# Attention and up-projection on four 32-row groups of TensorE, in an order written by a planner

## The chip, the core and the metric

The kernel runs on one core of a Trainium2 chip. A core has five engines that work side by side, each through its own queue in order: TensorE (PE in the profile; PEld is its weight load), VectorE (DVE), ScalarE (ACT), GpSimd (POOL) and SyncE (SP, which here only starts transfers). Operands lie in SBUF, 128 partitions wide; matmul results go to PSUM, in banks of 128 x 512 fp32. A matmul has a stationary operand, loaded first (up to 128 rows x 128 columns), and a moving operand that streams past it. The metric is the device time of one launch in microseconds.

## The reference

One sequence of S = 2048 rows, width D = 448, H = 16 heads of 28, hidden width F = 1792, all fp32:

```python
qkv = x @ wqkv                                   # split into q, k, v by head
scores = q @ k^T * 28 ** -0.5
a = (softmax(scores) @ v) @ wo                   # per head, heads side by side
b = (gelu(x @ w_gate) * (x @ w_up)) @ w_down     # tanh form of gelu
g = sigmoid((x * gate_w).sum(-1, keepdims=True))
return g * a + (1 - g) * b
```

Products are taken nearly in fp32: each operand is split into a high part (`hi`, type fp32r) and the rest (`lo`), and hi x hi, hi x lo and lo x hi are added up in PSUM.

## The kernel before

The program has three stages, one after the other on TensorE.

**Stage 1, projections.** x is split into the SBUF tensor `X` (7 blocks of 128 rows: three of hi, three of lo, and one that holds hi and lo of the last 64 rows). q and k are computed transposed, a tile of 128 rows x 512 tokens by 11 matmuls (`PAIRS` lists which block of x meets which block of the weights), evicted as hi and lo and stored to DRAM (`qkd`). Then 16 tiles of v follow (`v_tile`, L209 evicts them on ACT), which stay in SBUF (`VA`).

**Stage 2, attention.** For each head, `Q` and `K` are read back as 4 x 28 rows (hi and lo stacked, so that one product of 114 rows gives all four partial products, with two rows more for a shift of the softmax). A score tile `sc` is 128 keys x 1024 queries: two matmuls of 128 x 512. ACT turns it into `pt` = exp(sc) (L352). A value turn (`values`) multiplies the `pt` of 8 key tiles with 32 columns of v each; four such matmuls stand in the four 32-column groups of the array, one for each quarter of the queries. There are two value turns in each head, 32 in all. Sums `o` are added on DVE (L364, L367). Since exp is slower than the scores, `up()` puts other matmuls between them: x @ w_up, and x @ w_gate for NB = 7 of 14 blocks of 128 hidden columns. Each block is 4 token blocks x 11 matmuls of 128 rows (`ps<-X,half`), evicted by DVE (L410) and stored to DRAM (`ud`). `RATES`, `ENDS` and `LATE` fix by hand how many of them follow each score tile.

When a head's sums are complete, `finish` and `divide` run a chain on POOL's queue: four stores of the denominators (`dend`, L373), one load of them over 128 partitions (`r`, L376), a reciprocal on DVE (L383), its store (`rdend`, L384), four broadcast loads (`rb`, L387), the product o * rb on POOL (L389), and four stores to `od` (L391). Each starts when the one ahead has landed.

**Stage 3, the down projection.** In pairs of hidden blocks and for each 512 tokens: `hidden` forms gelu(gate) * up and splits it into `hl`; `down` multiplies it with the rows of w_down (`pd`, 24 matmuls of 448 columns) and DVE adds the result into `acc` (L514). For the 7 gate blocks that stage 2 left, the gate product is computed here (`pg`, 11 matmuls each); for the others it is loaded from `ud`. Gelu runs on ACT (L494), the product with `u` on DVE (L495), the hi copy on ACT (L496), the rest `lo` on DVE (L497). Rows of w_down are split by `load_f` (L478 on ACT, L479 on DVE). Near the end `load_o` and `project` multiply the attention output with `wo`.

All matmuls go through the helper `mm` (L54), so the profile gives them one line; tiles tell them apart. `pin` keeps an instruction at its place in program order; what is not pinned is placed by the framework's scheduler, but each engine then runs its queue strictly in that order.

Of the kernel before, what the change touches and what calls it, by code (L numbers as in the profile page):

```python
# [25 lines left out]
ENDS = (7, 15)  # L26
LATE = 1
RATES = (2,) * 13 + (1,) * 3
NB = 7
ORDER = (7, 8, 0, 9, 1, 10, 2, 11, 3, 12, 4, 13, 5, 6)  # L30
# [3 lines left out]
NR = 4 * DH + 2  # L34
# [9 lines left out]
PAIRS = [(b, w) for b in range(3) for w in (b, 4 + b)] + [(4 + b, b) for b in range(3)] + [(3, 3), (3, 7)]  # L44


@with_exitstack
def gated_mix(ctx: ExitStack, tc: tile.TileContext, xT, wqk, wvg, wg, wu, wd, wo, sel, ident, out):
# [18 lines left out]
    X = keep.tile([P, 7, S], F32R, name="X")  # L67
    fw = ctx.enter_context(tc.tile_pool(name="fw", bufs=2))
    attn = ctx.enter_context(ExitStack())
    vp = attn.enter_context(tc.tile_pool(name="vp", bufs=1))  # L70
# [6 lines left out]
    halves = {}  # L77

    def load_half(src, f, key, hi, mark=lambda ins: ins):
        raw = fw.tile([P, 4, P], F32, name="hraw", bufs=1)  # L80
        w = fw.tile([P, 8, P], F32R, name="half", bufs=2)
        mark(nc.sync.dma_start(out=raw, in_=src[f]))
        mark(hi(w[:, 0:4], raw))
        mark(nc.vector.tensor_tensor(w[:, 4:8], raw, w[:, 0:4].bitcast(F32), OP.subtract))
        halves[key, f] = w


    with ExitStack() as ph:
        wq = ph.enter_context(tc.tile_pool(name="wq", bufs=1))
        st = ph.enter_context(tc.tile_pool(name="st", bufs=1))  # L90
        wp = ph.enter_context(tc.tile_pool(name="wp", bufs=1))
# [140 lines left out]
        nc.vector.tensor_tensor(sq, sq, sq, OP.mult)  # L232
        for i in range(4):
            v_tile(i)
            if i in (1, 3):

                load_half(wu, i // 2, "u", nc.vector.tensor_copy, pin)
# [6 lines left out]
        for i in range(4, NT):  # L244
            last = v_tile(i)
            if i == NT - 4:
# [19 lines left out]
    kq = attn.enter_context(tc.tile_pool(name="kq", bufs=1, reuse_waits="tile"))  # L266
    heads = [tuple(kq.tile([P, S], F32R, name=f"{x}{i}") for x in "QK") for i in range(2)]
    for Q, K in heads:
        pin(nc.gpsimd.memset(K[96:].bitcast(F32), 1.0))

        pin(nc.gpsimd.memset(Q[96:].bitcast(F32), 0.0))

    def load_q(dst, h):
        for j, a in enumerate((0, 0, 1, 1)):
            nc.sync.dma_start(out=dst[j * DH:(j + 1) * DH].bitcast(F32), in_=qkd[a, h * DH:(h + 1) * DH])

    def load_k(dst, h):
        for j, a in enumerate((0, 1, 0, 1)):
            nc.sync.dma_start(out=dst[j * DH:(j + 1) * DH].bitcast(F32), in_=qkd[a, D + h * DH:D + (h + 1) * DH])

    load_k(heads[0][1], 0)
    load_q(heads[0][0], 0)


    bounded = nc.values_load(flag[0:1, 0:1], min_val=0, max_val=1)
    with tc.If(bounded < 1, label="rows"):
        with ExitStack() as ph:
# [5 lines left out]
            for h in range(H):  # L293
                Q = gp.tile([4 * DH, S], F32R, name="gQ")
                K = gp.tile([4 * DH, S], F32R, name="gK")
                load_q(Q, h)
                load_k(K, h)
# [18 lines left out]
    gp0 = ctx.enter_context(tc.tile_pool(name="gp0", bufs=1, side="right"))  # L316
    def by_act(o, i):
        return nc.scalar.activation(o, i, AF.Copy)


    with ExitStack() as ph:
        pp = ph.enter_context(tc.tile_pool(name="pp", bufs=17))
        op = ph.enter_context(tc.tile_pool(name="op", bufs=2))
        psc = ph.enter_context(tc.tile_pool(name="psc", bufs=3, space=PSUM))
        pss = ph.enter_context(tc.tile_pool(name="pss", bufs=1, space=PSUM))
        PT, ends = {}, []
        sums = {}

        last, block = 0, None

        def place():
            nonlocal last
            last = 1 - (last if block is None else block)
            return last, pss.tile([P, TB], F32, name=f"ps{last}")

        def load_head(h):
            Q, K = heads[h % 2]
            if h:  # L340
                load_k(K, h)
                load_q(Q, h)
            nc.sync.dma_start(out=Q[4 * DH:NR].bitcast(F32), in_=shd[h])

        def scores(h, kt, half):
            Q, K = heads[h % 2]
            sc = psc.tile([P, 1024], F32, name="sc")
            for c in range(2):
                mm(sc[:, c * 512:(c + 1) * 512], K[:, kt * P:(kt + 1) * P],
                   Q[:, half * 1024 + c * 512:half * 1024 + (c + 1) * 512], True, True)  # L350
            pt = pp.tile([P, 1024], F32, name="pt")
            nc.scalar.activation(pt, sc, AF.Exp, scale=SCALE)  # L352
            PT[h, kt, half] = pt

        def values(tiles):

            _, po = place()
            for n, (h, kt) in enumerate(tiles):
                for j in range(4):
                    mm(po[j * 32:(j + 1) * 32], VA[:, kt, h * VC:h * VC + 32],  # L360
                       PT[h, kt, j // 2][:, (j % 2) * 512:(j % 2 + 1) * 512], n == 0, n == len(tiles) - 1)
            if h in sums:
                o = sums.pop(h)
                nc.vector.tensor_tensor(o, po, o, OP.add)  # L364
            else:
                sums[h] = o = op.tile([P, 512], F32, name="o")
                nc.vector.tensor_copy(o, po)  # L367
            if kt == NKT - 1:
                finish(h, o)

        def finish(h, o):
            for j in range(4):
                nc.gpsimd.dma_start(out=dend[h:h + 1, j * 512:(j + 1) * 512],  # L373
                                    in_=o[j * 32 + DH:j * 32 + DH + 1])
            r = op.tile([P, S // P], F32, name="r")
            nc.gpsimd.dma_start(out=r, in_=dend[h].rearrange("(p n) -> p n", p=P))  # L376
            ends.append((h, o, r))

        def divide():

            while ends:
                h, o, r = ends.pop()
                nc.vector.reciprocal(r, r)  # L383
                nc.gpsimd.dma_start(out=rdend[h].rearrange("(p n) -> p n", p=P), in_=r)  # L384
                rb = op.tile([P, 512], F32, name="rb", bufs=1)
                for j in range(4):
                    nc.gpsimd.dma_start(out=rb[j * 32:(j + 1) * 32],  # L387
                                        in_=rdend[h:h + 1, j * 512:(j + 1) * 512].to_broadcast([32, 512]))
                nc.gpsimd.tensor_tensor(o, o, rb, OP.mult)  # L389
                for j in range(4):  # L390
                    nc.gpsimd.dma_start(out=od[h * DH:(h + 1) * DH, j * 512:(j + 1) * 512],  # L391
                                        in_=o[j * 32:j * 32 + DH])

        def up():

            nonlocal last, block
# [19 lines left out]
        def fill(n):  # L416
            for _ in range(n):
                next(filler, None)
# [192 lines left out]
```

## Time and profile before

| | us |
|---|---|
| median of 3 runs | 1036.96 (1036.67 to 1038.16) |
| the profiled execution | 1038.66 |
| its span, first to last instruction | 1036.8 |
| PE busy | 1030.6 (99%) |
| ACT busy | 603.3 (58%) |
| DVE busy | 325.7 (31%) |
| POOL busy | 195.9 (19%) |
| weight loads (PEld) busy | 737.6 (71%) |
| share of the chain that ended last on PE | 88% |

A busy share close to 100% does not say that TensorE is at its peak: the end of a matmul is modelled, and two that follow each other overlap in the record. How fast it goes is read from the distance between the starts of two matmuls. A group's row reads: line, engine, operation, output<-inputs, shapes, count | busy us, mean ns of one | idle us of that engine just ahead of it, and what ended that idle time.

### The profile page before, as it was taken

Reading aid. Unit: us, or ns where it says so; the run is one execution under the profiler, and the core shown is the slowest. Engines: PE = TensorE matmul, PEld = TensorE weight load, DVE = VectorE, ACT = ScalarE, POOL = GpSimd, SP = SyncE. Lnnn points to the kernel's source line nnn. Section 1 sums busy time; section 2 is a strip of 40 time slices with the busy share of each in tenths; the row PEclk is TensorE's granted clock in tenths of the full one; section 3 lists DMA queues with packets and bytes.
Section 4 is the critical chain, followed back from the end, with each engine's and each line's share of the span. In section 5 each row is a group of like instructions: output and inputs, shape, how many; then the busy total and the mean of one; then the engine's idle time right before and its main releaser. Section 6 shows DMA issues by size and latency. Waiting matters only on the chain.

```text
span 1036.8 us, 14751 instructions
## 1 busy us (share of the span) xinstructions
PE 1030.6 (99%) x5671; PEld 737.6 (71%) x5671; DVE 325.7 (31%) x519; ACT 603.3 (58%) x742; POOL 195.9 (19%) x294
## 2 busy tenths in 40 slices
PE   9999999999999999999999999999999999999998
PEld 7889865666566556655665566556666888888997
DVE  5452011111111111111111111111113687777756
ACT  4332575777577757775777677667763344333322
POOL 6322003021130221211312302202111200001221
PEclk9999999999999999999999999999999999999999
DMA  6865324324234233344242342423124645443553
GB/s 222 315 262 145 78 87 113 103 71 124 75 93 118 83 103 83 88 124 112 71 113 87 96 113 71 115 76 107 53 79 149 175 140 161 140 120 82 160 170 118
DMA packets 59964, 124.25 MB, mean 120 GB/s; under 512 B 11472, under 2 KB 18384, under 8 KB 56272
## 3 DMA queue, kind: packets, MB, share of 16 engines
q1 hardware_dynamic: 50672, 109.99, 35.9%
q0 software_dynamic: 8384, 12.47, 4.5%
q8 instruction: 47, 0.77, 0.3%
q10 hardware_dynamic: 832, 0.79, 0.3%
q14 instruction: 29, 0.24, 0.1%
HBM read 78.64 MB, written 44.56 MB: 119 GB/s over the span
## 4 chain that ended last, share of the span: by engine, by line
PE 88%; DVE 0%; issue 0%
PE ps L54 42%; PE sc L54 23%; PE pd L54 17%; PE pg L54 7%; DVE y L517 0%
## 5 line engine op out<-in xcount | busy, mean ns | idle before, releaser
L352 ACT ACTIVATE pt<-sc 128x1024 f32<-128x1024 f32 x512 | 475.0, 1074 | 188.7 <-PE sc L54 188.4
L54 PE MATMUL sc<-Q,K 128*128 128x512 f32 x1024 | 319.7, 393 | 0.0
L54 PE MATMUL ps<-X,half 128*128 128x512 f32 x924 | 289.7, 391 | 0.1
L54 PEld LDWEIGHTS sc<-Q,K 128*128 128x128 f32 x1024 | 188.8, 188 | 65.2 <-issue 26.0
L54 PE MATMUL ps<-pt,V 128*32 128x512 f32 x2048 | 226.4, 594 | 0.0
L54 PEld LDWEIGHTS ps<-X,half 128*128 128x128 f32 x924 | 173.3, 188 | 38.8 <-issue 1.4
L54 PEld LDWEIGHTS ps<-pt,V 128*32 128x32 f32 x2048 | 63.4, 110 | 145.6 <-issue 144.5
L54 PE MATMUL pd<-w,hl 128*128 128x448 f32 x672 | 140.7, 366 | 0.0
L410 DVE COPY u<-ps 128x512 f32<-128x512 f32 x84 | 57.9, 689 | 256.6 <-PE ps L54 256.5
L54 PEld LDWEIGHTS pd<-w,hl 128*128 128x128 f32 x672 | 126.0, 188 | 11.5
L373 POOL DMA_DIRECT2D dend<-o x64 | 31.8, 505 | 417.7 <-DVE o L364 414.8
L496 ACT ACTIVATE hl<-g 128x512 fp32r<-128x512 f32 x56 | 35.4, 632 | 89.8 <-DVE g L495 80.1
L54 PE MATMUL pg<-X,half 128*128 128x512 f32 x308 | 74.3, 391 | 0.0
L54 PE MATMUL pqk<-X,WQK 128*128 128x512 f32 x308 | 72.8, 399 | 0.9 <-ACT X L152 0.8
L54 PEld LDWEIGHTS pqk<-X,WQK 128*128 128x128 f32 x308 | 59.3, 193 | 14.7 <-ACT X L152 1.5
L54 PEld LDWEIGHTS pg<-X,half 128*128 128x128 f32 x308 | 57.9, 188 | 11.6
L514 DVE SCALAR_TENSOR_TENSOR acc<-pd,gate,acc 128x448 f32<-128x448 f32 x80 | 53.6, 680 | 21.6 <-PE pd L54 21.6
L367 DVE COPY o<-ps 128x512 f32<-128x512 f32 x16 | 11.1, 691 | 148.4 <-PE ps L54 89.2
L364 DVE TENSOR_TENSOR o<-ps,o 128x512 f32<-128x512 f32 x16 | 11.1, 691 | 147.8 <-PE ps L54 147.8
L170 ACT ACTIVATE hl<-pqk 128x512 fp32r<-128x512 f32 x28 | 16.7, 598 | 42.5 <-PE pqk L54 40.5
L497 DVE TENSOR_TENSOR hl<-g,hl 128x512 fp32r<-128x512 f32 x56 | 38.4, 686 | 9.6 <-ACT hl L496 8.5
L495 DVE TENSOR_TENSOR g<-g,u 128x512 f32<-128x512 f32 x56 | 38.0, 686 | 10.5 <-ACT g L494 9.8
(73 smaller groups left out, 528.9 us busy)
## 6 DMA issues: line engine op xcount, KB each, us to landing
ud<-u SPq DMA_DIRECT2D x84, 256.0 KB
qkd<-hl SPq DMA_DIRECT2D x28, 512.0 KB
K<-qkd SPq DMA_DIRECT2D x64, 224.0 KB
Q<-qkd SPq DMA_DIRECT2D x64, 224.0 KB
u<-ud SPq DMA_DIRECT2D x56, 256.0 KB
gs<-ud SPq DMA_DIRECT2D x28, 256.0 KB
rb<-rdend POOLq DMA_DIRECT2D x64, 64.0 KB, 2.9
raw<-in_xT SPq DMA_DIRECT2D x14, 256.0 KB
```

What stands on the lines that cost most here:

```text
L54: return pin(nc.tensor.matmul(o, lhsT, rhs, start=start, stop=stop))
L170: pin(nc.scalar.activation(hl[:, 0], p, AF.Copy))
L352: nc.scalar.activation(pt, sc, AF.Exp, scale=SCALE)
L364: nc.vector.tensor_tensor(o, po, o, OP.add)
L367: nc.vector.tensor_copy(o, po)
L373: nc.gpsimd.dma_start(out=dend[h:h + 1, j * 512:(j + 1) * 512], in_=o[j * 32 + DH:j * 32 + DH + 1])
L410: nc.vector.tensor_copy(u, p)
L495: pin(nc.vector.tensor_tensor(g, g, u, OP.mult))
L496: nc.scalar.activation(hl[:, 0], g, AF.Copy)
L497: nc.vector.tensor_tensor(hl[:, 1], g, hl[:, 0].bitcast(F32), OP.subtract)
L514: nc.vector.scalar_tensor_tensor(acc[:, t], p, g1, acc[:, t], OP.mult, OP.add)
```

## The change

The array is used as four groups of 32 rows. Each group holds its own stationary operand of 32 rows x 128 columns, reads its own 32 partitions of the moving operand and writes its own PSUM bank.

- **Scores.** `K` and `Q` of a head are laid out four times, one copy in each group of 32 partitions (28 rows, and two for the shift), hi and lo side by side; group r holds half of the keys and half of the queries. A score tile is now 128 keys x 512 queries, and consists of three products on one group (hi x hi, lo x hi, hi x lo; `product`). lo x lo, which the stacked form had, is left out. There are 1024 such tiles, 3072 quarter products.
- **x @ w_up and x @ w_gate.** x is kept as `X32`: 14 blocks of 32 rows for each of hi and lo, token block r in group r. A hidden block is 14 x 3 = 42 products on each of the four groups (`cross`), one group for each token block. 27 of 28 blocks (all of w_up, 13 of w_gate, NB = 13) lie beside the scores, in `chunks` of half a block; the last gate block (`PG`) comes as 42 steps ahead of stage 3.
- **Order.** `plan()` runs ahead of the build over a table of durations in ns (`STEP` and the others) and writes the order of every product, exp, copy, eviction and value turn. A step is at most one product on each group. Four banks of PSUM are for scores and four for the groups' sums (which the value turns share). Where a score bank is to come free sooner, DVE copies the scores to SBUF (`aside`, 364 of 1024) and ACT takes exp of the copy later. A group's sum may be evicted half done (`clear`) and added up in SBUF.
- **Value turns** take 4 key tiles, 64 turns in all.
- **Stage 1** also loads x once more in the new layout and splits it (`load_x32`, `split_x32`: ACT and DVE, between the v tiles), and loads and splits the first chunks of weights.
- **Stage 3** forms no gate product but the one in `PG`. The product gelu * u moves from DVE to POOL. `u` and `gs` get 6 buffers instead of 3. Pools of stage 3 lie on the space of stage 2's pools.

On PE, in the middle of attention, with the products `sc` of a score tile, the products `ps` of x with the up and gate weights, and a value turn (`ps<-pt,V`). Before, a stretch around a value turn:

```order
L54 MATMUL ps_2976<-X,half 128x512
L54 MATMUL sc<-Q_961,K_962 128x512 x2
L54 MATMUL ps_3009<-pt,V 32x512 x32
L54 MATMUL sc<-Q_961,K_962 128x512 x2
L54 MATMUL ps_2976<-X,half 128x512 x2
```

The same kind of place after the change:

```order
L205 MATMUL sc_9884<-Q_1081,K_1080 128x512
L205 MATMUL ps_9736<-X_697,w_9252 128x512
L205 MATMUL ps_9806<-X_697,w_9252 128x512
L205 MATMUL ps_9899<-pt,V 32x512 x16
L205 MATMUL ps_9618<-X_697,w_9687 128x512
L205 MATMUL sc_9934<-Q_1081,K_1080 128x512
L205 MATMUL sc_9936<-Q_1081,K_1080 128x512
L205 MATMUL sc_9938<-Q_1081,K_1080 128x512
```

Pairs of whole-array products have become rows of products on different groups, and a turn has 16 value matmuls in the program where it had 32.

On POOL, at the end of attention (o, r, rb: the last head's sum, its denominators, their reciprocals). Before, the head's chain is followed by the loads for `project`:

```order
L389 TENSOR_TENSOR o<-o,rb 128x512 [waits DMASW2_49,DMASW3_49,DMASW1_49,DMASW0_49]
L391 DMA od<-o 28x512 [waits Pool_49]
L391 DMA od<-o 28x512
L391 DMA od<-o 28x512 [waits DMASW6_49]
L533 DMA oraw<-od 128x3x512 [waits DMAHW3_49,DMAHW4_49,DMAHW2_49,DMAHW5_49,DMAHW1_49,DMAHW6_49,DMAHW0_49,DMAHW7_49,DVE_49,PE_49]
```

After it:

```order
L566 TENSOR_TENSOR o<-o,rb 128x512 [waits DMASW2_49,DMASW3_49,DMASW1_49,DMASW0_49]
L568 DMA od<-o 28x512 [waits Pool_49]
L568 DMA od<-o 28x512
L568 DMA od<-o 28x512 [waits DMASW6_49]
L695 TENSOR_TENSOR g<-g,u 128x512 [waits DMAHW3_49,Activation_49]
L695 TENSOR_TENSOR g<-g,u 128x512 [waits DMAHW4_49,PE_49,Activation_49]
```

The products gelu * u of stage 3 now stand behind the last head's chain.

On ACT, at the seam of stages 2 and 3 (w, draw: rows of w_down; pg, gs: gate products). Before:

```order
L478 ACTIVATE w_8342<-draw 128x448 [waits DMAHW7_49,PE_49,Activation_49]
L478 ACTIVATE w_8352<-draw 128x448 [waits DMAHW0_49]
L494 ACT_TABLE_LOAD [waits DMAHW3_49,DMAHW2_49,DMAHW5_49,PE_49]
L494 ACTIVATE g<-pg 128x512 [waits Pool_49]
L478 ACTIVATE w_8377<-draw 128x448 [waits DMAHW2_49]
```

After:

```order
L680 ACTIVATE w_17450<-draw_17451 128x448 [waits DMASW4_49,DMASW5_49,DMASW3_49,DMASW6_49,DMASW2_49,DMASW7_49,DMASW1_49,DMAHW6_49,DMASW0_49,Pool_49]
L694 ACT_TABLE_LOAD [waits PE_49]
L694 ACTIVATE g<-pg_17089 128x512 [waits Activation_49]
L694 ACTIVATE g<-gs 128x512 [waits DMAHW5_49,Activation_49]
L696 ACTIVATE hl_17277<-g 128x512 [waits Pool_49]
```

The split of the fourth block of w_down rows, ahead of the first gelu, now waits for DMAs of POOL's queue (DMASW: these are the last head's, its stores to `od` among them), because its tile lies where the last head's sum lay.

The core of the diff:

```diff
-NB = 7
-ORDER = (7, 8, 0, 9, 1, 10, 2, 11, 3, 12, 4, 13, 5, 6)
+NB = NF - 1
+ORDER = (NF - 1,) + tuple(range(NF - 1))
+TURN = 4
+LEAD = 8
+FIRST = 16
+RUN = 30
+STEP, READ, SEEN = 227, 270, 200
+EXP, EXP_OUT, COPY, BACK = 480, 620, 690, 100
+VALUES, INTO, OUTOF = 857, 90, 200
...
+def plan(count, parted=2, loaded=3):
...
+    def step():
+        nonlocal now
+        did = []
+        for r in range(4):
+            if score[r]:
+                i, key, b, n, _ = score[r]
+                ops.append(("score", r, key, n, b))
...
+            elif cross_ready(r):
+                ops.append(["cross", r, pos[r], not held[r], False])
...
+        now += STEP
...
+    def split_x32(u):
+        c, k, n = UNITS[u]
+        a, raw = slice(7 * c + k, 7 * c + k + n), xraw[u][:, 0:n]
+        pin(nc.scalar.activation(X32[:, 0, a], raw, AF.Copy))
+        pin(nc.vector.tensor_tensor(X32[:, 1, a], raw, X32[:, 0, a].bitcast(F32), OP.subtract))
+        if len(xraw) < len(UNITS):
+            load_x32()
...
         for i in range(4, NT):
             last = v_tile(i)
+            if 4 <= i < 12:
+                split_x32(i - 4)
...
+        def product(r, key, n, b):
...
+            mm(sc[b], K[group(r), int(n == 1), k * P:(k + 1) * P],
+               Q[group(r), int(n == 2), q * TB:(q + 1) * TB], n == 0, n == 2)
...
+        def cross(r, n, first, last):
...
+            mm(ps[r], halves[n // 21][group(r), int(j == 1), i], X32[group(r), int(j == 2), n // 21 % 2 * 7 + i],
+               first, last)
...
+        def values(i, r):
+            h, k0 = turns[i]
+            po = pss.tile([P, TB], F32, name=f"ps{r}")
+            for kt in range(k0, k0 + TURN):
+                for j in range(4):
+                    mm(po[j * 32:(j + 1) * 32], VA[:, kt, h * VC:h * VC + 32], PT.pop((h, kt, j)),
+                       kt == k0, kt == k0 + TURN - 1)
...
+        for kind, *what in steps:
+            does[kind](*what)
         divide()
...
-            u = tp.tile([P, TB], F32, name="u")
+            u = tp.tile([P, TB], F32, name="u", bufs=6)
...
-                pg = psg.tile([P, TB], F32, name="pg")
-                for i, (x, w) in enumerate(PAIRS):
-                    mm(pg, halves["g", f][:, w], X[:, x, s], i == 0, i == len(PAIRS) - 1)
+                pg = PG[tb]
             pin(nc.scalar.activation(g, pg, AF.Gelu_apprx_tanh))
-            pin(nc.vector.tensor_tensor(g, g, u, OP.mult))
+            nc.gpsimd.tensor_tensor(g, g, u, OP.mult)
...
+        PG = [psg.tile([P, TB], F32, name=f"pg{r}") for r in range(4)]
+        for k in range(42):
+            i, j = divmod(k % 21, 3)
+            w = halves[2 * NF + 2 * NB + k // 21]
+            for r in range(4):
+                g = group(r)
+                mm(PG[r], w[g, int(j == 1), i], X32[g, int(j == 2), k // 21 * 7 + i], k == 0, k == 41)
```

More of the change, by code (lines that the diff above doesn't have):

```diff
@@ L33 @@
 LAG = 6
-NR = 4 * DH + 2
 VC = DH + 1
@@ L74, in gated_mix @@
     nc.gpsimd.memset(VA[:, :, H * VC:], 0.0)
[L77 to L85, printed above, removed]
[L88 to L91 removed]
+    rows = ctx.enter_context(ExitStack())
@@ L245, in gated_mix @@
             last = v_tile(i)
+            if 4 <= i < 12:
+                split_x32(i - 4)
+            if i in (12, 13):
+                for part in range(4):
+                    split_chunk(i - 12, part)
+                load_chunk()
             if i == NT - 4:
@@ L325, in gated_mix @@
+        op = ph.enter_context(tc.tile_pool(name="op", bufs=2, side="right"))
+        psc = ph.enter_context(tc.tile_pool(name="psc", bufs=1, space=PSUM))
         pss = ph.enter_context(tc.tile_pool(name="pss", bufs=1, space=PSUM))
[L326 to L369, printed above, removed]
+        PT, ends, sums = {}, [], {}
```

397 lines of the change are left out of this document (293 added, 104 removed).

## The prediction

> **What bounds the kernel now.** First I cut the span into the three stages by the busy time of each engine in four stretches (0 to 78.4 q and k, to 115.4 v, to 790.4 attention, then the down projection):
>
> ```profile
> 0.00:78.40 78.40, 76.04 (x316) 61.67 (x317) 41.21 (x64) 30.66 (x53) 30.27 (x30) 1.00 0.74 264
> 78.40:115.40 37.00, 37.00 (x205) 33.83 (x204) 5.51 (x16) 9.69 (x31) 7.05 (x4) 1.00 0.41 102
> 115.40:790.40 675.00, 674.85 (x3998) 425.35 (x3998) 103.55 (x173) 476.61 (x517) 126.28 (x225) 1.00 0.34 94
> 790.40:1036.80 246.40, 242.75 (x1157) 216.75 (x1155) 175.42 (x268) 86.36 (x141) 32.32 (x35) 1.00 0.49 146
> ```
>
> Columns: stretch, length, busy time (and count) of PE, PEld, DVE, ACT, POOL, granted clock, DMA share, GB/s. PE is never idle from the first tile on, the clock is granted in full, and ACT has 198 us to spare in attention. So the time is the number of PE steps times the length of each. The lengths come from PE's timeline, a stretch between two value turns, by the distance of starts:
>
> ```profile
> 305.08 0.73 PE L54 MATMUL sc<-Q,K 128*128 128x512 f32 x2
> 305.65 0.63 PE L54 MATMUL ps<-X,half 128*128 128x512 f32 x2
> ...
> 307.04 0.63 PE L54 MATMUL sc<-Q,K 128*128 128x512 f32 x2
> ...
> 316.12 0.61 PE L54 MATMUL sc<-Q,K 128*128 128x512 f32 x2
> ...
> 318.17 0.63 PE L54 MATMUL sc<-Q,K 128*128 128x512 f32 x2
> 318.73 1.49 PE L54 MATMUL ps<-pt,V 128*32 128x512 f32 x12
> ```
>
> From 307.04 to 316.12 lie 20 rows of two: 9.08 / 40 = 0.227 us for a whole-array product of 512 columns. The value turns show in the weight loads, and two more groups of loads give a load's price:
>
> ```profile
> 300.25 0.13 PEld L54 LDWEIGHTS ps<-pt,V 128*32 128x32 f32 x4 [0.30 <-issue]
> ...
> 304.12 0.13 PEld L54 LDWEIGHTS ps<-pt,V 128*32 128x32 f32 x4 [0.30 <-issue]
> ```
>
> ```profile
> L54 PEld LDWEIGHTS sc<-Q,K 128*128 128x128 f32 x1024 | 188.8, 188 | 65.2 <-issue 26.0
> ...
> L54 PEld LDWEIGHTS ps<-pt,V 128*32 128x32 f32 x2048 | 63.4, 110 | 145.6 <-issue 144.5
> ```
>
> ```profile
> L54 PEld LDWEIGHTS pr<-selt,sq x14: 81/81/82, 87.8 to 88.2; 128*1 128x1 f32 x14
> ```
>
> Nine groups of four from 300.25 to 304.12 give 0.43 us for four column-group products. Their four loads take 63.4 / 512 = 0.124 us together and 0.110 each: they run side by side. A load of 1 column takes 81 ns and one of 128 columns 188, so 107 ns are the columns. The last value group starts at 304.12 + 0.43 and ends at 304.98; the first score starts at 305.65 - 0.454 = 305.20: 0.22 us out of a turn. Into it: 318.73 - 318.17 - 0.454 = 0.11. Together 0.33 for each turn.
>
> **The change, part by part.**
>
> *Steps.* Before: 1024 score products, 924 beside them and 308 in the last stage, 2,256 in all. After: 3072 + 4 x 1134 quarter products, 1,902 full steps if every place were filled, and 42 for the last gate block. The list that the planner writes has 2,009 steps (1,664 with four products, 274 with three, 59 with two, 12 with one), so 2,051 with the block. What a step of four groups takes, no row shows. From below: four groups side by side in the value turns, 0.43 for two passes of 512, or 0.215. From above: four loads one after another, 4 x 0.107 = 0.428. I take 0.227, the row of the same width, type and column count, whose load is hidden as well: 205 steps fewer, **-46.5 us**.
>
> A rule speaks against it. The Trainium skill (TensorE: Matmul & The Clock Gate, Part 3) states that a weight load overlaps matmuls in flight only where the row group differs. Here 188 ns of load and a 512-column product fit into 0.227 us on the same rows, so this trace disagrees for the whole array; no run so far shows it for groups. By that rule a group's load would follow its own product, 0.227 + 0.107, and the sum would be +220 us.
>
> *Value turns.* The same matmuls, but 64 turns: 32 x 0.33 = **+10.4**.
>
> *Stage 1.* ACT and DVE get x once more, in units of 128 x 1024.
>
> ```profile
> L352 ACT ACTIVATE pt<-sc 128x1024 f32<-128x1024 f32 x512 | 475.0, 1074 | 188.7 <-PE sc L54 188.4
> ...
> L497 DVE TENSOR_TENSOR hl<-g,hl 128x512 fp32r<-128x512 f32 x56 | 38.4, 686 | 9.6 <-ACT hl L496 8.5
> ```
>
> ACT 1.1, DVE 2 x 0.69 = 1.4, then the load two units on may start: 512 KB at 264 GB/s (first stretch) is 2.0, and 1.9 to land (the od row below). That is 6.4 for two units, 3.2 each, while a v tile takes 37.0 / 16 = 2.3. Six units wait, 6 x 0.9 = 5.4, and PE's second PSUM buffer covers a tile: **+3** (0 to 6).
>
> *ACT and DVE in attention.* A turn lasts 2,009 / 64 x 0.227 + 3.4 + 0.33 = 10.9 us. 16 exps of half the width cost 16 x 0.49 (475.0 / 512 = 0.93 halved, and a start) = 7.8; DVE has 5.7 copies and 2.5 evictions (364 and 163 in 64 turns) and a sum at 0.69, and 2 us of weight splits, 8.4. Neither is the bound, but a score waits for one of four banks: **+2** (0 to 15).
>
> *The seam.* This is where the gain goes. The last head's chain ran off PE's path before:
>
> ```profile
> 790.70 1.98 POOL L373 DMA_DIRECT2D dend<-o  x4 [32.25 <-DVE o L364]
> 797.10 0.56 POOL L376 DMA_DIRECT2D r<-dend  x1 [4.43 <-DMA dend<-o]
> ...
> 812.97 1.39 POOL L389 TENSOR_TENSOR o<-o,rb 128x512 f32<-128x512 f32 x1 [7.02 <-DMA rb<-rdend]
> 814.65 2.04 POOL L391 DMA_DIRECT2D od<-o  x4 [0.29 <-POOL o L389]
> ```
>
> ```profile
> L391 POOL DMA_DIRECT2D od<-o x64 | 32.6, 516 | 4.7 <-POOL o L389 4.7
> L387 POOL DMA_DIRECT2D rb<-rdend x64 | 32.1, 507 | 28.0 <-DMA rdend<-r 28.0
> L373 POOL DMA_DIRECT2D dend<-o x64 | 31.8, 505 | 417.7 <-DVE o L364 414.8 <-issue 2.9
> L389 POOL TENSOR_TENSOR o<-o,rb 128x512 f32<-128x512 f32 x16 | 20.5, 1282 | 43.0 <-DMA rb<-rdend 43.0
> ...
> L384 POOL DMA_DIRECT2D rdend<-r x16 | 9.0, 562 | 51.9 <-DVE r L383 51.9
> L376 POOL DMA_DIRECT2D r<-dend x16 | 8.9, 554 | 51.0 <-DMA dend<-o 51.0
> ```
>
> ```profile
> DMA to landing us min/median/max: 1.8/1.9/7.1
> ```
>
> From the first `dend` store to the end of the last `od` issue it took 816.69 - 790.70 = 26.0 beside the bulk loads of stage 3; an average head, busy times and idle times of these groups / 16 (the idle ahead of `dend` left out), takes 19.7. A store lands 1.9 after its issue, 1.4 after the issue ends: 21.1 to 27.4. I take 22, near the average, since the `wo` load that stood in the way of `rb` comes later now. After the change POOL's gelu * u stands behind this chain, and ACT's split of the fourth w_down block waits for the landing, ahead of every gelu. Then follow on ACT and POOL:
>
> ```profile
> L494 ACT ACTIVATE g<-pg x28: 578/590/600, 794.4 to 978.8; 128x512 f32<-128x512 f32 x28
> ...
> L494 ACT ACT_TABLE_LOAD  x1: 1283/1283/1283, 793.1 to 793.1; - x1
> ```
>
> ```profile
> L496 ACT ACTIVATE hl<-g 128x512 fp32r<-128x512 f32 x56 | 35.4, 632 | 89.8 <-DVE g L495 80.1
> ```
>
> split 0.6, table 1.28, gelu 0.59, product 1.28, copy 0.63, and 0.5 allowed for handovers: 4.9. Ahead of it 0.22 out of the turn, 0.69 sum and 0.3 to the first store, 1.2. So the first `pd` comes 28.1 after the last value product; the gate block covers 42 x 0.227 + 0.22 = 9.7. PE is idle for **+18.4** (17.5 to 23.8), and the first pair of `hl` comes apart: **+1.0**. A PE that rested is slow, as at the start:
>
> ```profile
> L54 PE MATMUL pqk<-X,WQK 128*128 128x512 f32 x11 | 5.4, 659 | 0.9 <-ACT X L152 0.8
> ```
>
> 11 matmuls in 5.4 us, where 0.227 each would be 2.5: **+2.5** (0 to 2.9).
>
> *Stage 3.* The rest is 848 `pd` products, as before:
>
> ```profile
> 800.52 4.87 PE pd L54 x24
> ```
>
> 24 are a step of 4.9 us. In it POOL has 2 x 1.28 = 2.6, DVE 6 x 0.69 = 4.1, and 1 MB of `u` and `gs` at 264 GB/s is 4.0: all hidden if nothing collides. But two rows show a collision:
>
> ```profile
> 955.50 2.95 DVE L541 TENSOR_TENSOR ohl<-oraw,ohr 64x512 fp32r<-64x512 f32 x1
> ```
>
> ```profile
> 954.40 3.50 POOL L542 TENSOR_TENSOR ohl<-oraw,ohl 128x1536 fp32r<-128x1536 f32 x1 [77.92 <-ACT ohl L538]
> ```
>
> A DVE operation on two SBUF tiles (0.69 in L497) ended only 0.55 after POOL's. The `lo` subtraction is of that kind, and POOL now works in half of each step. Slack is 0.8 a step: **+2** (0 to 43, each subtraction waiting out a whole product: 4.1 + 2.6 - 4.9 = 1.8, 24 steps). The `load_o` work on POOL delays products behind it, with one step of lead: **+2** (0 to 10).
>
> *Sum.* -46.5 + 10.4 + 3 + 2 + 18.4 + 1.0 + 2.5 + 2 + 2 = -5.2, a span of 1031.6 against 1036.8. The profiled execution took 1038.66, 1.70 above the median of 1036.96; taken off the median, **1032**.
>
> **Rivals.**
> - *A step is longer (slower).* Each ns costs 2.05 us, and 229.5 ns use the gain up. Loads of 32 x 128 on four groups might slow each other: 240 ns gives +26.7, 1058. For: these loads have 128 columns, not 32. Against: four beside each other cost 14 ns more than one. 13%.
> - *DVE bounds stage 3 (slower)*, by the collision at its full price: +41, 1073; it decides from 0.4 us of wait a subtraction on. 10%.
> - *The groups do not run side by side.* Loads hidden behind nothing give +220, 1251; loads in a row 0.428, +412, 1444. 12%. The Trainium skill (same page, Part 3) gives a measured speed-up of 3.07 for four row groups. By that figure an estimate of the step is 0.296, and the time 1173.
> - *A step is shorter*, 0.215 as in the value turns: -24.6, 1007. 13%.
> - *The seam is hidden*, if the chain's landing comes within the 9.7 us of the gate block: -20.9, 1011. The 19.7 of an average head speaks against it. 9%.
>
> **Chances.** The forecast has 43%, on it 30 faster, 7 within 0.2% (about what a measurement of this kernel can tell from no change), 6 slower. With 13 + 9 faster and 13 + 10 + 12 slower: 52% faster, 7% same, 41% slower. The range 1004 to 1080 leaves out the groups that do not run side by side and little else.
>
> **What would show it.** PE's timeline in attention: four products starting together every 0.227 us. PE idle of 17 to 24 us ahead of the first `pd`, ended by ACT's `hl`, behind ACT's split that waits for `od`. Some 0.33 around each turn. DVE's `lo` in stage 3 at a mean over 0.9 would speak for the collision; PE idle inside turns, for the planner's durations being wrong.

## The result and the profile after

The changed kernel takes 1095.03 us (median of 4 runs, 1094.38 to 1099.5) beside 1036.88 us before (1036.67 to 1038.16): a ratio of 1.0567, 95% interval 1.0538 to 1.0597. It is 58 us slower, where 5 us faster were forecast; 1095 lies above the range. The profiled execution took 1094.65 us, with a span of 1092.9.

The same stretches as before but the first, which hardly changed, with the last stage in three (the gate block, PE's rest, the down projection):

```profile
78.40:123.40 45.00, 37.96 (x206) 32.72 (x204) 13.79 (x24) 16.37 (x41) 2.89 (x3) 1.00 0.53 138
123.40:844.90 721.50, 712.47 (x9659) 477.74 (x9659) 492.75 (x828) 523.18 (x1026) 130.48 (x226) 0.99 0.43 126
844.90:854.80 9.90, 9.83 (x172) 8.65 (x168) 1.95 (x4) 1.06 (x2) 3.08 (x6) 1.00 0.03 6
854.80:881.30 26.50, 0.01 (x1) 0.01 (x1) 1.28 (x3) 4.18 (x6) 7.30 (x11) 0.57 0.57 178
881.30:1092.90 211.60, 188.00 (x848) 162.18 (x848) 141.59 (x199) 78.29 (x128) 94.73 (x75) 0.96 0.54 169
```

PE, hardly ever idle before, now rests at four places. Against the prediction's own terms, in us of the span:

| | predicted | measured | missed by |
|---|---|---|---|
| v stage ends | 118.4 | 123.4 | +5.0 |
| attention lasts | 700.9 | 721.5 | +20.6 |
| gate block | 9.7 | 9.8 | +0.1 |
| PE idle at the seam | 18.4 | 26.6 | +8.2 |
| first `pd` to last | 180.4 | 207.7 | +27.3 |
| after the last `pd` | 3.8 | 3.9 | +0.1 |

(The predicted 180.4 are 172.9 for the 848 products, which is about what the stage before leaves without its 308 gate products, and the 7.5 of the terms for the first pair, the cold PE, the collision and `load_o`; attention is what the forecast span of 1031.6 leaves.) In attention the products of the four groups do start together, and the next four follow:

```profile
303.04 0.40 PE L205 MATMUL ps<-X,w 32*128 32x512 f32 x2
303.06 0.42 PE L205 MATMUL sc<-Q,K 32*128 32x512 f32 x2
303.26 0.38 PE L205 MATMUL ps<-X,w 32*128 32x512 f32 x1
303.28 0.43 PE L205 MATMUL sc<-Q,K 32*128 32x512 f32 x3
...
303.79 0.38 PE L205 MATMUL ps<-X,w 32*128 32x512 f32 x1
304.10 3.64 PE L205 MATMUL ps<-pt,V 128*32 128x512 f32 x32
307.67 0.49 PE L205 MATMUL sc<-Q,K 32*128 32x512 f32 x1
...
308.01 0.40 PE L205 MATMUL ps<-X,w 32*128 32x512 f32 x1
```

```profile
844.89 9.84 PE L205 MATMUL pg<-X,w 32*128 32x512 f32 x168
```

The gate block gives the price without turns: 42 steps, and from the first start to the last (9.84 - 0.38) / 41 = 0.2307 us each. The 3072 weight loads for `sc` take 183 ns each at a mean. A value turn takes 307.67 - 304.10 = 3.57. The four rests (the seam, the boundaries of the pairs in stage 3, x in stage 1, the start of attention) begin so in the view of waits:

```profile
PE pd L205 <- ACT hl L696: 37.5, 7, 26.6
...
ACT w L680 <- DMA draw<-in_wd: 33.0, 4, 25.0
...
ACT w L680 <- PE pd L205: 19.6, 5, 4.1
...
ACT X L248 <- DMA xraw<-in_xT: 14.1, 5, 4.9
...
PE sc L205 <- DMA Q<-shd: 9.0, 2, 6.0
```

Columns: us in all, times, longest. Of the 37.5 us in which PE waits for `hl`, 26.6 are the seam; five of the other six are nearly 2 us each. Their cause stands on ACT and PE around one of them:

```profile
903.27 0.58 ACT L680 ACTIVATE w<-draw 128x448 fp32r<-128x448 f32 x1 [4.05 <-PE pd L205]
903.76 0.62 ACT L694 ACTIVATE g<-gs 128x512 f32<-128x512 f32 x1
...
905.75 0.63 ACT L696 ACTIVATE hl<-g 128x512 fp32r<-128x512 f32 x1 [0.91 <-POOL g L695]
```

```profile
906.43 1.84 PE L205 MATMUL pd<-w,hl 128*128 128x448 f32 x3 [1.95 <-ACT hl L696]
```

ACT waits 4.05 us for PE to free a `w` buffer; the gelu, POOL's product and the copy stand behind it, and PE then waits for them. At the seam, SP, ACT and POOL in turn:

```profile
846.06 1.96 POOL L551 DMA_DIRECT2D dend<-o  x4 [9.61 <-DVE o L635]
...
861.30 2.05 POOL L568 DMA_DIRECT2D od<-o  x4 [0.29 <-POOL o L566]
```

```profile
864.82 0.80 SPq L687 DMA_DIRECT2D u<-ud  x2
...
871.20 0.33 SPq L678 DMA_DIRECT2D draw<-in_wd  x1
```

```profile
871.24 0.58 ACT L680 ACTIVATE w<-draw 128x448 fp32r<-128x448 f32 x1 [24.96 <-DMA draw<-in_wd]
```

The last `od` store is issued by 863.35, 17.3 us after the chain began, and lands at 864.68 by the view of the chain that ended last: 18.6 us, where 22 were taken. But SP's first `u` load goes out only at 864.82, and the `draw` loads come among those of `u`.

### The profile page after: what moved, and what is told of

It reads as the page before. It is cut to its first block, busy times and chain, and to the rows that moved or that the text cites. A ratio compares the mean times of both kernels' runs of the same rounds, so it can differ in the third digit from the quotient of the medians.

```text
span 1092.9 us, 28107 instructions
## 1 busy us (share of the span) xinstructions
PE 1024.8 (94%) x11191; PEld 741.9 (68%) x11191; DVE 692.5 (63%) x1121; ACT 654.2 (60%) x1255; POOL 271.4 (25%) x352
## 4 chain that ended last, share of the span: by engine, by line
PE 67%; issue 9%; POOL 6%; DMA 5%; DVE 1%; ACT 1%; SPq 0%; POOLq 0%; DVEq 0%; ACTq 0%
PE ps L205 45%; PE sc L205 20%; POOL g L695 4%; PE pd L205 2%; DMA oraw<-od 2%; DMA gs<-ud 1%; DVE hl L697 0%; ACT g L694 0%; POOL ohl L751 0%; SPq L262 0%; DMA u<-ud 0%; DVE ohl L750 0%; DMA draw<-in_wd 0%; DVE WO L737 0%; DMA dend<-o 0%
## 5 line engine op out<-in xcount | busy, mean ns | idle before, releaser
L205 PE MATMUL ps<-X,w 32*128 32x512 f32 x4536 | 480.9, 393 | 0.7 <-ACT gate L431 0.7
L594 ACT ACTIVATE pt<-sc 128x512 f32<-128x512 f32 x660 | 353.3, 608 | 194.8 <-PE sc L205 191.9
L205 PE MATMUL sc<-Q,K 32*128 32x512 f32 x3072 | 434.2, 404 | 9.0 <-DMA Q<-shd 9.0
L205 PEld LDWEIGHTS ps<-X,w 32*128 32x128 f32 x4536 | 387.1, 184 | 29.9 <-issue 10.1
L205 PEld LDWEIGHTS sc<-Q,K 32*128 32x128 f32 x3072 | 306.2, 183 | 76.1 <-issue 52.6
L598 DVE COPY pt<-sc 128x512 f32<-128x512 f32 x364 | 245.3, 689 | 62.9 <-PE sc L205 58.0
L594 ACT ACTIVATE pt<-pt 128x512 f32<-128x512 f32 x364 | 221.5, 646 | 0.8 <-DVE pt L598 0.8
L205 PE MATMUL pd<-w,hl 128*128 128x448 f32 x672 | 150.2, 380 | 41.1 <-ACT hl L696 37.5
L205 PEld LDWEIGHTS pd<-w,hl 128*128 128x128 f32 x672 | 128.1, 193 | 62.6 <-ACT hl L696 40.2
L635 DVE TENSOR_TENSOR o<-ps,o 128x512 f32<-128x512 f32 x48 | 33.2, 692 | 110.6 <-PE ps L205 110.6
L695 POOL TENSOR_TENSOR g<-g,u 128x512 f32<-128x512 f32 x56 | 73.3, 1314 | 87.7 <-ACT g L694 80.8
L275 DVE TENSOR_TENSOR w<-wraw,w 128x512 fp32r<-128x512 f32 x112 | 72.2, 684 | 0.0
```

The lines of the kernel that those rows point to most:

```text
L205: return pin(nc.tensor.matmul(o, lhsT, rhs, start=start, stop=stop))
L275: pin(nc.vector.tensor_tensor(w[:, 1, a], raw[:, a], w[:, 0, a].bitcast(F32), OP.subtract))
L594: pin(nc.scalar.activation(PT[key], PT[key] if b is None else sc[b], AF.Exp, scale=SCALE))
L598: pin(nc.vector.tensor_copy(PT[key], sc[b]))
L635: pin(nc.vector.tensor_tensor(sums["o"], po, sums["o"], OP.add))
L695: nc.gpsimd.tensor_tensor(g, g, u, OP.mult)
```

## Experiments

Each is the changed kernel with one edit, unless it says otherwise; times are medians beside runs of the kernel before on the same chip. That kernel took 1036.9 to 1038.2 us in them, so a difference of about 1 us between two runs says nothing.

**The start of attention.** `load_shift` of head 0 on POOL's queue:

```diff
-            nc.sync.dma_start(out=Q[32 * r + DH:...], in_=shd[h, :, half])
+            eng = nc.gpsimd if h == 0 else nc.sync
+            eng.dma_start(out=Q[32 * r + DH:...], in_=shd[h, :, half])
```

> Edit: the four loads that put the shift rows into Q of head 0 go out on POOL's queue instead of SP's; nothing else. Theory: PE's 9.0 us of waits for Q at the start of attention (3.0 ahead of 130.3, 6.0 ahead of 137.1) come from SP's queue, where these loads stand behind the raw weight chunks, which wait for DVE's split. Then both waits shrink to under 3 us together, attention ends 5 to 9 us earlier, and the kernel takes 1086 to 1090 us. Rival: PE would next wait for the second weight chunk, which DVE finishes only at 131 us, and for the branch on the flag; then the waits change their name (PE on DVE's w instead of DMA's Q) and the kernel takes 1092 to 1096.

1087.05 us, ratio 1.0481 (1.0463 to 1.0500): 8.0 us less. The theory holds: of 9.0 us of waits, 3.0 are left, 2.5 for which the profile names no engine (the branch on the flag stands there) and half a us for `Q`:

```profile
129.11 0.47 PE L205 MATMUL sc<-Q,K 32*128 32x512 f32 x1 [2.50 <-issue]
```

**Stage 1.** `load_k(0)` and `load_q(0)` with `eng` in the same way:

> Edit: as in the run with the shift rows on POOL, and K and Q of head 0 loaded on POOL's queue as well. Theory: stage 1 is 7 us longer than before since the x loads for X32 stand behind the 16 loads of K and Q on SP's queue (84 to 95 us); with these elsewhere the v tiles wait for ACT at most 2 us, the first product of attention starts at 116 to 119 instead of 123.4, and the kernel takes 5 to 7 us less than the run with the shift rows alone. Rival: the x loads are slow by themselves (512 KB through two buffers), and stage 1 stays within 2 us of 123.4.

1085.11 us, 1.9 us less than with the shift rows alone, which is within the spread of the two (1081.5 to 1085.4, 1084.3 to 1088.8). Attention starts at 119.72 instead of 122.68 in that run, 3.0 us earlier: neither theory nor rival. K and Q, which hold SP's queue for 11 us ahead of x in the changed kernel, are under half of the delay; for the rest x's loads through two buffers are late by themselves (in this run PE still waits 1.80 and 1.55 us for ACT, and ACT for x). In the changed kernel:

```profile
83.95 7.15 SPq L290 DMA_DIRECT2D K<-qkd  x8
91.20 3.48 SPq L298 DMA_DIRECT2D Q<-qkd  x8
94.78 3.56 SPq L242 DMA_DIRECT2D xraw<-in_xT  x8
```

Three buffers were not tried.

**The pairs' boundaries in stage 3.**

```diff
-            n = len(WD) % 4
+            n = len(WD) % 5
```

> Edit: five buffers for the split w_down blocks instead of four. Theory: the six idle times of about 2 us on PE at the pairs' boundaries in stage 3 come from ACT's w split, which waits for the products of the pair before to free its buffer and holds up the gelu behind it. Then these idle times go (12 us), the granted clock does not fall behind them (some 3 us more), and the kernel takes 1078 to 1084 us. Rival: POOL's product, 1.3 us each and in a chain with ACT's copy and DVE's subtraction, is late by itself, by the loads of u or by contention with DVE; then the idle times stay over 1 us at the boundaries, and the kernel takes 1089 to 1095.

1080.97 us, ratio 1.0426 (1.0408 to 1.0443): 14.1 us less, in the theory's range. The five idle times of 1.95 to 1.98 us are gone; where PE stood still from 904.5 to 906.4, it now runs through:

```profile
898.75 11.53 PE L205 MATMUL pd<-w,hl 128*128 128x448 f32 x55
```

The down projection is 15.2 us shorter (first to last `pd` 192.5, was 207.7):

```profile
882.20:1078.50 196.30, 180.40 (x848) 161.32 (x848) 135.20 (x198) 77.68 (x127) 100.09 (x75) 0.98 0.59 181
```

PE's idle time fell from 211.6 - 188.0 = 23.6 to 15.9, and its busy time by 7.6, at a granted clock of 0.98 instead of 0.96. Other waits of PE have come up in their place, 7.6 us in three waits for DVE's evictions of `acc`.

**The seam, by the place of the pools.**

```diff
+        gp1 = ...tile_pool(name="gp1", ...)
+        tp = ...tile_pool(name="tp", ...)
+        hp = ...tile_pool(name="hp", ...)
         ap = ...
         acc = ap.tile([P, NT, D], F32, name="acc")
-        hp = ...
-        tp = ...
-        gp1 = ...
```

> Edit: in the last stage the pools are opened in another order (w and draw first, then tp, hp, and acc last), so that tp's buffers lie on space of V and the exponentials and no longer on that of the last head's o. Theory: of the 26.6 us in which PE is idle at the seam, 15 to 16 come after the landing of od: SP's first u load waits for it, and the w_down loads behind it on SP's queue keep ACT's splits and with them the gelu back. Then ACT's gelu comes before 862, POOL's product right behind its last od issue (863.4 to 864.7), the first pd at about 866, and the kernel takes 1078 to 1081 us. Rival: ACT's splits are late by the two draw buffers and by the transfers themselves (5 us each), whatever stands ahead of them; then PE's idle time falls by under 5 us, to 1090 to 1094.

1089.72 us, 5.3 us less. SP's `u` loads go out early, as the theory says, but the idle time falls only to 20.5 us, for a reason that neither had: beside the bulk loads POOL's chain for the last head takes 27.2 us (844.85 to 872.06) instead of 17.3, and the product is queued behind it:

```profile
844.79 0.85 SPq L687 DMA_DIRECT2D u<-ud  x2
```

```profile
844.85 1.97 POOL L551 DMA_DIRECT2D dend<-o  x4 [9.50 <-DVE o L635]
...
872.08 2.49 POOL L695 TENSOR_TENSOR g<-g,u 128x512 f32<-128x512 f32 x2
```

So both are needed: the loads off `o`'s space and the product off POOL's queue. The same pools with the first pair's products on DVE, and with four `draw` buffers:

```diff
-            nc.gpsimd.tensor_tensor(g, g, u, OP.mult)
+            if f in order[:FC]:
+                pin(nc.vector.tensor_tensor(g, g, u, OP.mult))
+            else:
+                nc.gpsimd.tensor_tensor(g, g, u, OP.mult)
```

> Edit: the pools in the other order, four draw buffers instead of two, and the products gelu * u of the first pair of blocks on DVE instead of POOL. Theory: with the pools alone the idle time at the seam fell only from 26.6 to 20.5 us, since POOL's chain for the last head, which then ran beside the bulk loads, took 27 us and held the product back on POOL's queue. With DVE's product it is held back only by the pinned reciprocal of the last head (858.3 in that run): product 0.7, copy 0.6, so the first pd at about 861, 7 us of idle time instead of 26.6, and 1073 to 1078 us. Rival: ACT's splits or u's landing are the next to be late; then PE is idle for over 12 us and the kernel takes 1081 us or more.

1089.15 us. The first `pd` comes at 862.77 after 8.3 us, as the theory has it, but the time does not: `acc` now lies on `o`, and DVE's first write of it waits for `od`.

```profile
862.77 6.82 PE L205 MATMUL pd<-w,hl 128*128 128x448 f32 x24 [8.33 <-ACT hl L699]
877.74 2.51 PE L205 MATMUL pd<-w,hl 128*128 128x448 f32 x4 [8.15 <-DVE acc L715]
```

```profile
876.91 0.68 DVE L715 TENSOR_SCALAR acc<-pd,gate 128x448 f32<-128x448 f32 x1 [12.27 <-DMA od<-o]
```

**All products on DVE**, where the kernel before had them, with five `w` buffers:

```diff
-            nc.gpsimd.tensor_tensor(g, g, u, OP.mult)
+            pin(nc.vector.tensor_tensor(g, g, u, OP.mult))
```

> Edit: five w buffers, as in the run of 1081 us, and all products gelu * u on DVE, where the kernel before had them. Theory: DVE then has 2 products, 2 lo subtractions and 4 evictions of 0.68 for each step of 24 products, 5.4 us against PE's 4.9, and becomes the bound: 28 x 5.4 and 31 us of other work are 183 us, 10 over PE's 173; with the waits that are left, 1083 to 1092 us. Rival: POOL's product, 1.41 us each in that run, and its contention with DVE (lo at a mean of 0.80 instead of 0.69) cost more than DVE's load; then the kernel takes 1070 to 1079 us, and lo goes back to a mean of 0.69.

1075.63 us, 5.3 less than the run with POOL's products: the rival. DVE does become the bound of the plain steps, 10.56 us for two where PE needs 2 x 4.86 (901.57 to 906.43 in the rows of before, further below):

```profile
954.16 10.00 PE L205 MATMUL pd<-w,hl 128*128 128x448 f32 x48 [0.56 <-DVE hl L697]
964.72 9.99 PE L205 MATMUL pd<-w,hl 128*128 128x448 f32 x48 [0.56 <-DVE hl L697]
```

But POOL's way cost more. DVE's `lo` with five buffers and POOL's products, and with DVE's:

```profile
L697 DVE TENSOR_TENSOR hl<-g,hl 128x512 fp32r<-128x512 f32 x56 | 44.3, 797 | 30.2 <-ACT hl L696 29.3
```

```profile
L697 DVE TENSOR_TENSOR hl<-g,hl 128x512 fp32r<-128x512 f32 x56 | 37.9, 682 | 0.8 <-ACT hl L696 0.3
```

The same edit by itself in the kernel before, the other way round (`pin(nc.vector...)` becomes `nc.gpsimd...`):

> Edit: in the kernel before, only the product gelu * u moves from DVE to POOL. Theory: there each step of stage 3 has 2.5 us of pg products beside the 4.9 of pd, so the longer chain (1.3 instead of 0.7 us) and the contention are covered, except where POOL's chain for the last head holds the first products back; 1037 to 1042 us, with lo on DVE at a mean of 0.75 or more. Rival: the product on POOL costs by itself, as the 5 us between the two runs with five w buffers say, or its queue behind the last head's od costs PE 10 us or more: 1043 to 1060 us.

1041.16 us beside 1038.16, ratio 1.0032 (1.0020 to 1.0045): 3 us slower, in the theory's range, with `lo` at a mean of 761 ns.

In the kernel before, 2.5 us of `pg` products stand ahead of each group of `pd` and cover the rest:

```profile
899.03 2.70 PE L54 MATMUL pg<-X,half 128*128 128x512 f32 x11
901.57 5.03 PE L54 MATMUL pd<-w,hl 128*128 128x448 f32 x24
906.43 2.69 PE L54 MATMUL pg<-X,half 128*128 128x512 f32 x11
```

**The order of the groups.** Two steps' products sorted by group where they follow each other (741 such pairs, 5,628 products):

```diff
+                for i in range(0, len(run), 2):
+                    paired += sorted([a for b in run[i:i + 2] for a in b], key=lambda a: a[1])
```

> Edit: in attention the quarter products of two steps are issued group by group (0 0 1 1 2 2 3 3) instead of step by step (0 1 2 3 0 1 2 3), wherever two steps follow each other without a turn or another engine's work planned between them; the same products. Theory: PE starts its products in the order of issue, and a second product of the same group starts 0.227 us after the first; then only neighbours of different groups run beside each other, eight products take up to 4 x 0.227 instead of 2 x 0.231 us, and with perhaps 700 pairs of steps the kernel takes 1250 to 1480 us. Rival: a product whose group is free passes one that waits, and the kernel stays within 10 us of 1095.

1104.73 us, 9.7 more: the rival. If products started in the order of issue, 741 pairs would have cost up to 741 x (4 x 0.227 - 2 x 0.231) = 330 us. A second product of a group waits while the others pass, so that four still run beside each other (the next start from 304.60 on):

```profile
304.37 0.38 PE L205 MATMUL ps<-X,w 32*128 32x512 f32 x1
304.38 0.38 PE L205 MATMUL sc<-Q,K 32*128 32x512 f32 x1
304.39 0.38 PE L205 MATMUL ps<-X,w 32*128 32x512 f32 x1
304.43 0.42 PE L205 MATMUL sc<-Q,K 32*128 32x512 f32 x1
```

That is 0.013 us a pair, where the order of issue would have cost 0.446. 9.7 us over 64 turns are 0.15 each; that this is the last group's lag at the end of a turn is argued from rows like these, not tested.

**Together.** The edits shown, the pools in the order `gp1`, `hp`, `tp`, `ap`, and

```diff
-                if n in (5, 6) and tb % 2 == 0:
-                    load_o((n - 5) * 2 + tb // 2)
+                if (n, tb) in ((4, 2), (5, 0), (5, 2), (6, 0)):
+                    load_o((n - 4) * 2 + tb // 2 - 1)
```

> Edit: all of it together: K, Q and the shift rows of head 0 on POOL's queue, five w buffers, four draw buffers, the pools in the other order (w and draw, hp, tp, acc), the products of the first pair on DVE, and the outputs of attention loaded one step earlier into two buffers. Theory: the costs found so far add up: 1095 - 10 (start and stage 1) - 14 (w buffers) - 19 (seam) - 4 (waits ahead of the projection) = 1048 us (1043 to 1054), so the kernel stays slower than before by about 1%. Rival: they hide behind each other, and the sum saves under 35 us, 1060 us or more.

1065.27 us: the rival. In that order of pools `u` lay on `o` again: SP's first `u` load waits for the last head's `od`, whose issue ends at 856.2, and the seam is back at 20.1 us.

```profile
857.87 0.80 SPq L690 DMA_DIRECT2D u<-ud  x2
```

With a gap below `acc`, so that nothing used early lies on `o`:

```diff
+        gap = ...tile_pool(name="gap", ...)
+        gap.tile([P, 9, TB], F32, name="gap")
         ap = ...
```

> Edit: as in the run with all of it together, but the pools in the order w and draw (three draw buffers), hp, tp, a gap of 18 KB that covers the last head's o, then acc, so that neither u nor acc lies on o; and all products gelu * u on DVE. Theory: of that run's 20.1 us at the seam 12 go, since neither SP's u loads nor DVE's first acc has to wait for od (the first pd at 8 to 9 us after the gate block, held back by DVE's reciprocal and ACT's splits), and DVE's product gives 5 as it did with five w buffers alone: 1046 to 1051 us. Rival: DVE, with 5.4 us of work for a step of 4.9, cannot make use of an earlier start, and what the seam saves comes back as waits of PE on DVE's hl: 1055 us or more.

1053.08 us, ratio 1.0148 (1.0132 to 1.0163). The seam came as forecast, 9.4 us; the sum is 2 us over the theory's range:

```profile
851.85 1.47 PE L205 MATMUL pd<-w,hl 128*128 128x448 f32 x2 [9.41 <-ACT hl L701]
```

The down projection took 193.7 us instead of the 186.9 of the other run with DVE's products, which gives back part of what the seam saved. The plain steps are not the reason: two take 10.56 us (925.56 to 936.12), as in that run. Some 6 us more stand between 946.7 and 972.9, where `load_o` now comes twice ahead of the first projection, and once in that run. DVE's `lo` lasts 3.92 us there instead of 0.68, from 964.76 to 968.68, and ends 0.55 after the operation of POOL beside it (964.63 to 968.13); it is the collision that the prediction describes. PE rests, and the granted clock is 0.57 from 957 to 965:

```profile
964.76 3.92 DVE L702 TENSOR_TENSOR hl<-g,hl 128x512 fp32r<-128x512 f32 x1
```

Another 1.5 us stand at a granted clock of 0.58 (902.7 to 906.8). That the earlier `load_o` costs this is read from the trace; no run has that edit alone. Two more runs tried to lift DVE's bound:

```diff
-            pin(nc.vector.tensor_tensor(g, g, u, OP.mult))
+            if f in order[:FC] or f % 2:
+                pin(nc.vector.tensor_tensor(g, g, u, OP.mult))
+            else:
+                nc.gpsimd.tensor_tensor(g, g, u, OP.mult)
```

> Edit: as in the run with the gap ahead of acc, but from the second pair of blocks on one of a step's two products is on POOL and one on DVE. Theory: with all products on DVE a step took 5.28 us in that run (10.56 for 48 products on PE), DVE's own work, against PE's 4.86 (19.44 for a pair of blocks with all products on POOL and five w buffers). With one on each, DVE has 4.7 and POOL 1.3 a step; the pairs without a projection come to 19.5 to 20.5 us instead of 21.1 to 22.5, those with one lose a little as well, and the kernel takes 1041 to 1047 us instead of 1053. Rival: POOL's product slows DVE's lo beside it (0.80 instead of 0.69 us) and lengthens the chain of its hl, so a step stays at 5.2 or more: 1050 to 1056 us.

1061.02 us, the rival and worse. POOL's product takes 1.50 us at a mean, longer than in the runs before it. Whether its length, its contention with DVE, or ACT's copy that waits for it ahead of the next gelu is the cause was not tested and stays open.

```diff
-                    if tb == 0 and k + 1 < NF:
+                    if tb == k - n * FC and k + 1 < NF:
```

> Edit: as in the run with one product on each engine, and the w_down block after the next is loaded in the second step of a pair instead of the first, with the first five splits of w held in the order written, so that only two splits stand ahead of the first gelu on ACT. Theory: the 9.4 us at the seam come from splits that wait for their draw loads (6.2 us for the fourth) beside the bulk loads; with two ahead only DVE's reciprocal of the last head holds the first product back (846.5 in that run): first pd at 848, 4 us less at the seam than with the splits ahead, 1037 to 1043 us. Rival: gelu and copy now alternate on ACT, each copy waits for its product, and the first steps lose what the seam gives: 1043 to 1050 us.

1061.82 us, outside both ranges, which counted on a faster run before. Beside that run the seam fell from 9.2 to 6.1 us and the down projection grew from 200.5 to 204.3: the first steps lost it again, as the rival has it. No run beats the kernel before; 1053 is the best.

## Why the prediction was wrong

- *Steps.* Right. The groups run side by side, at 0.2307 us a step, not 0.227: 2,009 x 0.0037 = 7.4 us missed. The three rivals of other step lengths are refuted, and so is the hidden seam. The Trainium skill (TensorE: Matmul & The Clock Gate, Part 3) states that a weight load overlaps products in flight only where the row group differs, that products start strictly in the order of issue, and that four groups were measured at a speed-up of 3.07. Here loads of 0.18 us on the same group fit into steps of 0.23, the reordered run shows products passing each other, and a step of four groups takes 0.2307 where one whole product takes 0.227. That is 3.9 times one group's work if a group's product alone takes as long as a whole one, which no run shows.
- *Value turns.* Of 721.5 - 9.0 us, 64 turns get 11.13 each; 2,009 / 64 = 31.4 steps are 7.24 and eight value groups 3.44, so 0.45 is left beside the 0.33 taken: 64 x 0.12 = 7.7 us. But this is a remainder, not the price of a turn. The rows around the turn shown give 0.13 to come out (3.57 - 3.44), 0.11 for a longer first step (307.67 to 308.01), and 0.08 to go in (303.79 to 304.10 is 0.31): 0.32, as taken. Some 2.3 us of the remainder are a cold PE at the start of attention, where the granted clock is 0.50 from 137.1, the end of the second wait, to 141.8, half of 4.7 us. Where the other 5 lie was not found. The 2 us taken for stalls of ACT and DVE did not come.
- *The start of attention.* No term of its own: 9.0 us of waits, of which the run with these loads on POOL's queue took away 6.0; its time fell by 8.0. I costed `load_shift` by nothing and did not follow SP's queue, on which the new raw chunks stand ahead of it, from 120.61 on. The second half of the shift rows shows it:

```profile
131.58 3.56 SPq L262 DMA_DIRECT2D wraw<-in_wu  x8
135.19 0.57 SPq L304 DMA_DIRECT2D Q<-shd  x2
```

- *Stage 1.* The mechanism was right, ACT late with x (14.1 us of waits for its loads); the term was mis-sized, 8 us instead of 3, since the third load stands behind 16 of K and Q.
- *The seam.* The chain was right, and its landing 3.4 us sooner than taken, 18.6 us instead of 22 (the rows of an average head add up to 19.6, not 19.7, on which nothing hangs). The step that failed is "then follow on ACT and POOL", 4.9 us from `od`'s landing to the first `pd`: it was 16.6. I let only ACT's fourth split wait for the landing; SP's queue waited as well, with two splits' loads behind it and some 5 us each to land. Cold PE cost what was said: 11 products in 4.7 us at a granted clock of 0.51.
- *Stage 3, "the rest is 848 `pd` products, as before".* The step that missed most, 27.3 us. ACT's wait for a `w` buffer was there before, five times and up to 6.8 us, but PE had 11 `pg` products ahead of every 24 `pd` then and did not wait for ACT:

```profile
ACT w L478 <- PE pd L54: 33.8, 5, 6.8
```

The change takes these products out of the stage: 15.2 us by the run with five buffers. In that run 19.6 us are left over the 172.9 of the products, 3.5 of them the cold PE and the first pair, as taken. The other 16.1 stand where collision and `load_o` were taken at 4 (up to 53): these terms were mis-sized by 12.1. With the products on DVE 14.0 are left in all, DVE being the bound. So 5.6 of the 16.1 go with POOL's products, net of what they cost DVE. The collision with these products is small, not the rival's: `lo` came to a mean of 0.78 in the changed kernel, beside 0.69 before and the 0.9 that was to show it, but it lasted 3.92 beside POOL's work for `load_o` in a later run. How the 16.1 divide between the longer chain, the contention and the waits ahead of the projections was not separated.

The sum: 5.0 for x, 9.0 at the start, 15.1 - 2 for steps and turns, 8.2 at the seam, 15.2 for the buffer and 12.1 for the rest of stage 3 are 62.6, where 61.3 us were missed. What the change saves in steps was right to 7 us in 46; what it uncovers was not looked for.

## What to carry over

When products leave a stage, ask of every engine in it which wait they covered, and size the stage again without them; "as before" is not a price for what is left. Follow each moved load through its queue, down to the first instruction ahead of it that waits for another engine, and ask on whose space its buffer lies. A fix at one wait brings out the next: of the 17 us that came off the seam, the new place of the pools gave 6, DVE's product and two more `draw` buffers 4 (8.3 + 8.2 us of rest were left), and the gap under `acc`, with the other edits beside it, the other 7.

## What the runs showed of the hardware

- Products of different row groups pass each other, as the reordered run shows: grouping 5,628 products by twos cost 9.7 us, where a strict order would have cost up to 330.
- The granted clock falls after some short rests and not after others of the same length. It reads 0.51 in the 4.7 us after the rest of 26.5 us, and 0.78 and 0.79 in the stretches with the rests ahead of 906.43 and 930.19 (1.95 and 1.96 us). It stays at 1.00 in the stretches with the three rests of 1.96 to 1.98 us ahead of 958.47, 982.02 and 1005.62. What decides between them was not tested.

```profile
881.30:886.00 4.70, 4.33 (x11) 3.52 (x12) 3.02 (x4) 2.27 (x4) 2.21 (x3) 0.51 0.85 286
...
904.40:908.00 3.60, 1.65 (x4) 1.09 (x4) 2.49 (x4) 1.59 (x3) 2.29 (x2) 0.78 0.51 114
```

```profile
980.00:1003.00 23.00, 20.57 (x95) 17.31 (x95) 16.64 (x26) 9.68 (x18) 10.28 (x8) 1.00 0.65 203
```

The Trainium skill (TensorE: Matmul & The Clock Gate, Part 1) puts the fall after an idle window of about 3.4 us; here it follows two of five rests of less than 2.

- DVE's subtraction on two SBUF tiles, 0.68 us by itself, took 3.92 beside an operation of POOL of 3.50 and ended 0.55 after it (the run with the gap). Beside POOL's products of 1.31 us its mean was 0.78 (the changed kernel).
- POOL's chain for the last head took 17.3 us on a quiet memory (DMA share 0.03 in the gate block, 0.19 from there to the landing) and 27.2 beside the bulk loads.
